# A mixture-of-experts step loop: one transfer for the first rows, shared layer 2 code, thin third tiles as fp32 column tiles, a width of 288

## The chip, the cores and the metric

The kernel runs on one core of one Trainium2 chip. The metric is the device time of one execution in microseconds (us). Five engines work at the same time and wait for each other on semaphores: TensorE (PE in the profile, PEld for its weight loads), VectorE (DVE), ScalarE (ACT), GpSimd (POOL) and SyncE (SP), which issues most transfers.

## The reference

```python
def reference(q, k, v, w_gate, w1, w2):        # 8 batches, 8 heads, 576 positions, 64 wide
    q_s = softmax(q, axis=-1); k_s = softmax(k, axis=2)
    kv = einsum('bhsd,bhse->bhde', k_s, v)
    x = einsum('bhsd,bhde->bhse', q_s, kv)     # then reshaped to 4608 rows x 512
    logits = x @ w_gate                        # 8 experts
    expert_idx = argmax(logits, axis=1)
    gate = softmax(logits)[arange, expert_idx]
    for e in range(8):                         # each row goes to one expert
        y[rows of e] = maximum(x[rows of e] @ w1[e], 0) @ w2[e]    # 512 -> 1024 -> 512
    return gate[:, None] * y
```

## The kernel before

The first 160 us compute the attention, batch by batch, and send every row with its gate and its number to a list in DRAM, `xs`, in which each expert has a region of its own. This part is written out by hand in `ORDER`; its last entries, `WE`, are matmuls on constants (L708) that keep TensorE running until the engines meet before the expert part.

The expert part works in steps of up to three tiles of 128 rows. In each step layer 1 (L1038) makes 8 blocks of 128 hidden units, 12 matmuls each, as wide as the step has rows; layer 2 (L1054) makes, tile by tile, 24 matmuls of 128x512. Both split every fp32 factor in a high and a low part and sum three products, so that each matmul takes one pass. ACT makes the high part of the hidden units from PSUM (`relus`, L1201), DVE the low part (`lows`, L1284). Once per expert ACT and DVE split the weights: W1 (L1240, L1325) in the last step of the expert before, W2 (L1208, L1287) in its own first step. Each finished tile is scaled by ACT (`yout`, L1192) and scattered by POOL (L1371).

The first 384 rows of expert 0 are done by code of their own (`first_l1` L740, `first` L1100). While it runs, POOL scatters the rows of the last batch one after another (L632), with a pause between; when they have landed, SP loads the rows of the first step of the loop (`xload`, L1430), and TensorE turns them (L1023) between the second and third tile of `first`. DVE meanwhile makes a table of the steps (`t5`, 41 small instructions); the other engines and SP read it as they walk over the steps, TensorE as it walks over the experts.

Counted on the inputs, the experts get 1150, 0, 542, 34, 595, 578, 0 and 1709 rows. The order of the loop is expert 0 (766 rows left), 7, 4, 5, 2, 3, then the two empty ones. A remainder of one or two full tiles and a thin one is done as a step of two tiles, 256 wide, and a last step of three tiles whose width goes by the rows of the third: 320 for up to 64 of them, else 352. So the loop has five steps of 384; then 256 and 320 for expert 7 (45 rows in the third tile), 256 and 352 for experts 4 (83) and 5 (66), 256 and 320 for expert 2 (30); and expert 3, with 34 rows, alone in a step of its own, `slim`. `slim` takes the fp32 factors unsplit and works in two column tiles of 64: its layer 2 (L1087) is 16 matmuls of 128x64 by 128x256, 32 in the profile, since each shows as two.

TensorE's loop (`pe_expert`) reads three fields of the table for an expert (`x.get`, L1009) and branches to one of five copies of the step's code, each with its own layer 2. After `slim` it still looks at the two empty experts (`again`, L1124).

SP (`body`, L1469 ff.) loads ahead: the rows of the step after next (`bload`), and in the first step of an expert the weights of the next one: W1 as soon as its room is free (L1465), W2 when the split of the old W2 is done (L1469, which waits on `sW2`).

Of the kernel before, what the change touches and what calls it, by code (L numbers as in the profile page):

```python
# [32 lines left out]
WARM_END = 10  # L33
# [20 lines left out]
L3 VG VH T0 L3 T1 PU L1 VL R5 RB RC RC L2 L3 L1 R5 RB RD RH RH RD L2 L3 PU PU WE WE WE WE WE WE WE WE WE WE  # L54
# [47 lines left out]
def attention_moe(ctx: ExitStack, tc: tile.TileContext, q, k, v, w_gate, w1, w2, xs, out):  # L102
# [35 lines left out]
    I0.GA = cst.tile([P, 3], F32, name="ga")  # L138
    I0.IX = cst.tile([P, 3], I32, name="ix")
# [100 lines left out]
    qthr = cst.tile([E, 2], F32, name="qthr")  # L240
# [15 lines left out]
    def consts():  # L256
# [17 lines left out]
        iota(qthr, pattern=[[Q, 2]], base=-2 * Q, channel_multiplier=0)  # L274
# [477 lines left out]
    def switch():  # L752
        ka.__exit__(None, None, None)
        right.pool = tc.tile_pool(name="it", bufs=1, side="right")
        it = right.it = right.pool.__enter__()
        W2H[0] = it.tile([P, NF, DM], F32R, name="w2h0")
        W2L[0] = it.tile([P, NF, DM], F32R, name="w2l0")
        hid = it.tile([P, 2, NF, 3 * P], F32R, name="hid")
        I0.HH, I0.HL = hid[:, 0], hid[:, 1]
        I0.RAW2 = it.tile([P, NF, DM], F32, name="raw2")  # L760
        I0.YT = [it.tile([P, DM], F32, name=f"yt{i}") for i in range(3)]
        I0.GS = it.tile([P, 3, 2], F32, name="gs")

    def tables():
# [3 lines left out]
        base, start, steps, total, cnt, tiles, threes, rank, own, ends, few, tiny = [  # L768
            small(name, [E, 1]) for name in ("base", "start", "steps", "total", "cnt", "tiles", "threes", "rank", "mykey", "ends", "few", "tiny")]
# [29 lines left out]
        MADE = 41  # L799

        def t5(sem):
# [24 lines left out]
            op('quarter', 'fill', lambda: STT(junk[:, 6, :2], qthr, 1.0, wide(fill, 2), op0=ALU.mult, op1=ALU.is_lt, accum_out=quarter))  # L826
# [6 lines left out]
            op('cut', 'big quarter', lambda: STT(cut, quarter, 2.0, big, op0=ALU.is_lt, op1=ALU.mult))  # L833
# [3 lines left out]
            op('on', 'at', lambda: TS(on, at, 0.0, None, op0=ALU.is_ge))  # L837
            op('last', 'cut quarter', lambda: STT(last, quarter, 1.0, cut, op0=ALU.add, op1=ALU.mult))
            op('tiny', 'few start', lambda: TS(tiny, start, 0.0, 3.0, op0=ALU.is_gt, op1=ALU.mult))
# [15 lines left out]
            op('F9', 'V1 V2 V3 V4 eq', lambda: TT(fld[:, 3 * MAXS:].rearrange("p (a w) -> p a w", a=NFLD), eq[:, None, :].to_broadcast([E, NFLD, TW]), V[:, :, None].to_broadcast([E, NFLD, TW]), op=ALU.mult))  # L855
            op('F0', 'on tiny', lambda: STT(part(fld, 0), on, tiny, part(fld, 0), op0=ALU.mult, op1=ALU.add))
# [62 lines left out]
    def first_gate():  # L919
        TS(I0.GA, XT[:, :, DM], EPS, None, op0=ALU.add)  # L920
        nc.vector.reciprocal(I0.GA, I0.GA)

    add("IM", y, 0, DVE, first_gate, [("IL", y, 0)])
    add("IN", y, 0, POOL, lambda: nc.gpsimd.tensor_copy(I0.IX, XT[:, :, DM + 1]), [("IL", y, 0)])
# [21 lines left out]
    with tc.tile_pool(name="qs", bufs=1, space=PSUM) as qs, tc.tile_pool(name="bx", bufs=1) as bx:  # L946
        I0.XB, I0.XX = bx.tile([P, 12, P], F32, name="xb"), bx.tile([P, NC, 12, 32], F32, name="xx")
        I0.RAW1 = bx.tile([P, NC, F], F32, name="raw1")
        I0.XG, I0.GN, I0.EP = [bx.tile([P, 3, 2], F32, name=n) for n in ("xg", "gn", "ep")]
# [16 lines left out]
def experts(nc, tc, g):  # L966
# [22 lines left out]
    sTH, sTQ, sTY, sTO, sTI, sTG, sXD, sTI2, sTZ = [sem(x) for x in ("sth", "stq", "sty", "sto", "sti", "stg", "sxd", "sti2", "stz")]  # L989
# [27 lines left out]
    def pe():  # L1017
# [42 lines left out]
        def step(w, tiles=3):  # L1060
            layer1(w)
            for u in range(tiles):
                layer2(u)

# [26 lines left out]

        def first(u):
# [19 lines left out]
        e.wait_ge(sX, 48)  # L1112
        for u in (2, 1, 0):
            tr(u, u == 0)
        e.wait_ge(sTC, 1)
        first(2)
        n, i, m2 = x.reg("n", 0), x.reg("i", 0), x.reg("m2", 0)

        def again(name, done=1):
            if done:  # L1120
                x.add("it", 1)
            x.add("n", 1)
            x.add("m2", 16)
            e.br_lt(n, E, "pe_expert", name)  # L1124
            at(name)
            e.br("pe_done")

        e.br("pe_expert")
        with nc.body("pe_expert", valid_engines=[e.engine]):
            body = nc.cur_bb  # L1130
            at = lambda name: nc.switch_bb(name, parent=body)
            r = e.snap(n, min_val=0, max_val=E - 1)
            wide = x.get(WIDE, r, 0, MAXS)
            rest = x.get(REST, r, 0, 5)
            small = x.get(SMALL, r, 0, 4)
            e.reg_mov(i, 0)
            e.br_cond(wide < 1, "pe_rest", "pe_full")
            at("pe_full")
            e.br("pe_wide")
            at("pe_wide")  # L1140
            step(3 * P)
            x.add("it", 1)
            x.add("i", 1)
            e.br_lt(i, wide, "pe_wide", "pe_wide_end")
            at("pe_wide_end")
            e.br("pe_rest")
            at("pe_rest")
            e.br_cond(rest < 1, "pe_none", "pe_some")
            at("pe_none")
            again("pe_out0", 0)  # L1150
            at("pe_some")
            e.br_cond(small < 1, "pe_last", "pe_small")
            at("pe_small")
            e.br_cond(small < 3, "pe_short", "pe_slim")
            at("pe_slim")
            slim()
            again("pe_out4")
            at("pe_short")
            step(2 * P, 1)
            e.br_cond(small < 2, "pe_small_end", "pe_second")  # L1160
            at("pe_second")
            layer2(1)
            e.br("pe_small_end")
            at("pe_small_end")
            e.br_cond(rest < 2, "pe_again", "pe_more")
            at("pe_again")
            again("pe_out1")
            at("pe_more")
            x.add("it", 1)
            e.br("pe_last")  # L1170
            at("pe_last")
            e.br_cond(rest < 4, "pe_320", "pe_352")
            at("pe_320")
            step(2 * P + 2 * Q)
            again("pe_out2")
            at("pe_352")
            step(2 * P + 3 * Q)
            again("pe_out3")
        nc.switch_bb("pe_done")

    def act():
# [6 lines left out]
        def yout(u, again=True):  # L1188
# [3 lines left out]
            m = e.activation(g.YT[u], g.PY[u], AF.Copy, scale=g.GA[:, u:u + 1]).wait_op(sPY[u], cu[u], GE)  # L1192
# [6 lines left out]
        def relus(split):  # L1199
            for f in range(NF):  # L1200
                e.activation(g.HH[:, f, :], g.PH[f][:, :W], AF.Relu).wait_op(sPH[f], it, GE).then_inc(sHH[f], 1)  # L1201
# [18 lines left out]
        def body(j):  # L1220
            kind = x.get(KD, j, 0, 4)
            with e.If(kind > 3):
                slim()
            with e.If(kind < 4):
                usual(j, kind)

        def usual(j, kind):
# [20 lines left out]
            with e.If(kind > 2):  # L1248
                yout(2)
# [15 lines left out]
    def dve():  # L1265
        x = Eng(nc.vector, "dve")
        e = nc.vector
        it, n1, n2, b80 = x.reg("it", 1), x.reg("n1", 1), x.reg("n2", 1), x.reg("b80", 84)

        def flip():  # L1270
            e.wait_ge(sXL, it)
            e.wait_ge(sGS, it)
            e.transpose(g.XX, g.XB.rearrange("p t (a c) -> p c t a", c=NC)).wait_op(sB, b80, GE)  # L1273
            e.tensor_tensor(g.GN, g.XG, g.EP, op=ALU.add).then_inc(sBT, 1)
            x.add("b80", 80)

        def evac():
            e.tensor_tensor(g.XL, xx, g.XH.bitcast(F32), op=ALU.subtract).wait_op(sXH, it, GE).then_inc(sXL, 1)
            e.reciprocal(g.GS[:, :, 0], g.GN[:, :, 0])
            e.tensor_copy(g.GS[:, :, 1], g.GN[:, :, 1]).then_inc(sGS, 1)  # L1280
# [19 lines left out]
        def body(j):  # L1300
            kind = x.get(KD, j, 0, 4)
            with e.If(kind > 3):
                slim()
            with e.If(kind < 4):
# [43 lines left out]
        e.memset(g.EP[:, :, 1], 0.0).then_inc(sB, 1)  # L1348
# [5 lines left out]
        e.tensor_tensor(g.GN, g.XT[:, :, DM:DM + 2], g.EP, op=ALU.add).wait_op(sB, 4, GE).then_inc(sEP, 1)  # L1354
# [176 lines left out]
```

## Time and profile before

| | |
|---|---|
| median of 3 runs | 582.86 us (582.41 to 583.08) |
| the profiled execution | 583.25 us, of which the span from its first to its last instruction is 581.5 us |
| TensorE busy | 553.1 us of the span |
| VectorE, ScalarE, GpSimd busy | 311.0, 245.1, 148.7 us |
| expert loop in the chain that ended last | from 187.26 us to the end |

The chain is the work that ended last, followed back step by step; an engine that stands in it from end to end sets the time there. The rows themselves stand in a section below.

### The profile page before, as it was taken

The page shows a single profiled execution, that of the slowest core. Times are in us where ns is not written, and L with a number is a line of the kernel's source. Part 1 is how long each engine was busy: PE and PEld are TensorE (multiplying, and loading weights), DVE is VectorE, ACT ScalarE, POOL GpSimd, SP SyncE. Part 2 cuts the span into 40 slices and gives each one's busy share as a digit, 9 for nine tenths or more (in the row PEclk, how much of TensorE's full clock was granted, in tenths as well). Part 3 has the DMA queues.
Part 4 walks back from the last instruction along what each step waited for, and adds up shares of the span by engine and source line. Part 5 has one row for each costly group of instructions (what it writes and reads, how often), then busy time and mean ns, then how long its engine had stood idle before and what let it go on. Part 6 is the DMA issues. An engine that isn't in the chain of part 4 may idle for free.

```text
span 581.5 us, 11677 instructions
## 1 busy us (share of the span) xinstructions
PE 553.1 (95%) x3880; PEld 490.6 (84%) x3881; DVE 311.0 (53%) x637; ACT 245.1 (42%) x498; POOL 148.7 (26%) x237
## 2 busy tenths in 40 slices
PE   6699898999998999999999999999999999999995
PEld 2577787898887989899898989898999889898983
DVE  5899997897671431635223242345735472745340
ACT  0699987787321222434131222242625242443331
POOL 4224698586651010110201001102010200110021
PEclk9799998999999999999999999999999999999998
DMA  8989999754568922072504011212570464054000
GB/s 282 315 265 318 322 343 372 244 186 154 205 240 241 268 57 52 12 217 92 167 0 90 18 34 58 60 33 72 187 199 0 121 233 108 18 174 178 18 36 9
DMA packets 64848, 87.21 MB, mean 150 GB/s; under 512 B 8750, under 2 KB 50222, under 8 KB 64176
## 3 DMA queue, kind: packets, MB, share of 16 engines
q1 hardware_dynamic: 58272, 66.70, 37.7%
q0 software_dynamic: 5968, 19.03, 8.8%
q10 hardware_dynamic: 576, 1.07, 0.5%
q8 instruction: 19, 0.31, 0.2%
q14 instruction: 13, 0.11, 0.1%
HBM read 64.83 MB, written 22.61 MB: 150 GB/s over the span
## 4 chain that ended last, share of the span: by engine, by line
PE 82%; DMA 6%; ACT 3%; DVE 2%; issue 2%; POOL 2%; SPq 1%; POOLq 0%; DVEq 0%; ACTq 0%
PE py L1054 33%; PE pt L1038 16%; PE ph L1038 16%; PE xp L512 4%; DMA vs<-in_v 3%; PE kv L375 3%; PE qT L494 2%; PE ph L740 2%; DMA kt<-in_k 1%; PE py L1100 1%; DMA xs<-xr,posi 1%; DMA xt<-xs 1%; PE xp L515 1%; PE pt L1087 1%; ACT vt L178 1%
## 5 line engine op out<-in xcount | busy, mean ns | idle before, releaser
L1054 PE MATMUL py<-w2h,hid 128*128 128x512 f32 x560 | 174.7, 389 | 0.0
L1054 PEld LDWEIGHTS py<-w2h,hid 128*128 128x128 f32 x560 | 105.2, 188 | 21.5
L1371 POOL DMA_INDIRECT out<-yt,ix x38 | 42.6, 1122 | 309.5 <-ACT yt L1192 303.8
L1054 PE MATMUL py<-w2l,hid 128*128 128x512 f32 x280 | 109.1, 390 | 0.0
L1284 DVE SCALAR_TENSOR_TENSOR hid<-pt,hid 128x384 fp32r<-128x384 f32 x52 | 28.8, 556 | 127.4 <-ACT hid L1201 127.2
L1192 ACT ACTIVATE yt<-py,ga 128x512 f32<-128x512 f32 x38 | 26.1, 687 | 139.8 <-PE py L1054 131.0
L1054 PEld LDWEIGHTS py<-w2l,hid 128*128 128x128 f32 x280 | 52.6, 188 | 10.6
L1284 DVE SCALAR_TENSOR_TENSOR hid<-ph,hid 128x384 fp32r<-128x384 f32 x52 | 29.0, 557 | 54.0 <-ACT hid L1201 54.0
L1201 ACT ACTIVATE hid<-ph 128x384 fp32r<-128x384 f32 x52 | 25.6, 492 | 60.2 <-PE ph L1038 60.2
L1201 ACT ACTIVATE hid<-pt 128x384 fp32r<-128x384 f32 x52 | 25.5, 491 | 59.7 <-PE pt L1038 46.9
L1273 DVE STREAM_TRANSPOSE xx<-xb 128x1536 f32<-128x1536 f32 x13 | 37.8, 2906 | 18.3 <-issue 18.3
L512 PE MATMUL xp<-kx,qTs 128*128 128x146 f32 x256 | 45.0, 318 | 2.5 <-ACT kx L413 2.4
L632 POOL DMA_INDIRECT xs<-xr,posi x36 | 37.7, 1047 | 25.0 <-issue 22.8
L512 PEld LDWEIGHTS xp<-kx,qTs 128*128 128x128 f32 x256 | 37.0, 199 | 5.5 <-ACT kx L413 2.9
L1038 PE MATMUL pt<-xh,w1h 128*128 128x384 f32 (+3 forms) x208 | 40.0, 314 | 0.0
L1038 PE MATMUL ph<-xl,w1h 128*128 128x384 f32 (+3 forms) x208 | 39.8, 313 | 0.0
L1038 PE MATMUL pt<-xl,w1h 128*128 128x384 f32 (+3 forms) x208 | 39.8, 313 | 0.0
L1038 PE MATMUL ph<-xh,w1h 128*128 128x384 f32 (+3 forms) x208 | 39.8, 313 | 0.0
L1038 PE MATMUL ph<-xh,w1l 128*128 128x384 f32 (+3 forms) x208 | 39.8, 313 | 0.0
L1038 PE MATMUL pt<-xh,w1l 128*128 128x384 f32 (+3 forms) x208 | 39.8, 313 | 0.0
L1038 PEld LDWEIGHTS pt<-xh,w1h 128*128 128x128 f32 x208 | 33.6, 189 | 1.6 <-issue 0.8
L1038 PEld LDWEIGHTS ph<-xh,w1h 128*128 128x128 f32 x208 | 33.4, 189 | 0.0
(258 smaller groups left out, 925.0 us busy)
## 6 DMA issues: line engine op xcount, KB each, us to landing
raw<-in_moe_w SPq DMA_DIRECT2D x10, 2048.0 KB, 8.2
kt<-in_k SPq DMA_DIRECT2D x14, 640.0 KB, 11.6
xb<-xs SPq DMA_DIRECT2D x32, 192.0 KB
qt<-in_q SPq DMA_DIRECT2D x8, 640.0 KB, 9.1
vs<-in_v SPq DMA_DIRECT2D x8, 640.0 KB, 7.9
qt<-in_q SPq DMA_DIRECT2D x8, 512.0 KB
vs<-in_v SPq DMA_DIRECT2D x8, 512.0 KB, 7.3
xt<-in_moe_w SPq DMA_DIRECT2D x8, 256.0 KB, 6.5
```

The lines of the kernel that those rows point to most:

```text
L375: nc.tensor.matmul(o.kv[i * D:(i + 1) * D, c, lo:lo + D + 1], o.kt[:, 2 * c + i, j, :], VT[b % 2][:, 2 * c + i, at:at + D + 1], start=Fals ...
L494: nc.tensor.transpose(qT[:, c, :], src[:, 2 * c:2 * c + 2, :].rearrange("p h d -> p (h d)"), ident)
L512: nc.tensor.matmul(xv[:, c, :KW], o.qT[i][:, c, :], kx[:, c, :], **flags)
L632: s = nc.gpsimd.indirect_dma_start(out=xs, out_offset=bass.IndirectOffsetOnAxis(ap=n.pi[:, t - t0:t - t0 + 1], axis=0), in_=xr[:, t, :], i ...
L740: m = nc.tensor.matmul(ph, wt[:, c, f * P:(f + 1) * P], xt[:, c, :], start=(n == 0), stop=(n == 3 * NC - 1))
L1038: m = e.matmul(ph, wt[:, c, f * P:(f + 1) * P], xt[:, c, :w], start=(n == 0), stop=(n == 3 * NC - 1))
L1054: m = e.matmul(g.PY[u], ht[:, f, u * P:(u + 1) * P], wt[:, f, :], start=(n == 0), stop=(n == 3 * NF - 1))
L1192: m = e.activation(g.YT[u], g.PY[u], AF.Copy, scale=g.GA[:, u:u + 1]).wait_op(sPY[u], cu[u], GE)
L1201: e.activation(g.HH[:, f, :], g.PH[f][:, :W], AF.Relu).wait_op(sPH[f], it, GE).then_inc(sHH[f], 1)
L1273: e.transpose(g.XX, g.XB.rearrange("p t (a c) -> p c t a", c=NC)).wait_op(sB, b80, GE)
L1284: e.scalar_tensor_tensor(g.HL[:, f, :], g.PH[f][:, :W], 0.0, g.HH[:, f, :].bitcast(F32), op0=ALU.max, op1=ALU.subtract).wait_op(sHH[f], it ...
L1371: e.indirect_dma_start(out=g.out, out_offset=bass.IndirectOffsetOnAxis(ap=g.IX[:, u:u + 1], axis=0), in_=g.YT[u], in_offset=None, bounds_c ...
```

## The change

The last `WE` matmuls are halved, from 10 to 5. SP loads the first step's rows in one transfer, with the row number read before it waits. TensorE waits for the table earlier and reads it ahead of the turning of these rows; in the loop it reads the next expert's three fields in each step, behind the first tile of layer 2. The loop has one copy of layer 2, to which the layer 1 of every width jumps. A third tile with up to 64 rows (`thin`) is done like `slim`'s layer 2: unsplit fp32 hidden units `HF`, which ACT copies in every step (128x64, 8 times), by an unsplit copy of W2, `RAWC`, which SP loads for each expert in its first step, ahead of the next expert's weights; its rows are scattered as halves. A width of 288 is added for up to 32 rows in the third tile. After `slim` TensorE is done. Two instructions are added to `t5`.

```diff
-WARM_END = 10
+WARM_END = 5
...
+            op('thin', 'cut quarter', lambda: STT(thin, quarter, 2.0, cut, op0=ALU.is_lt, op1=ALU.mult))
...
+            op('F0', 'F2 thin', lambda: STT(part(fld, 0), part(fld, 2), thin, part(fld, 0), op0=ALU.mult, op1=ALU.add))
...
+        def thin():
+            e.wait_ge(sYT[2], cu[2])
+            x.add("c2", 1)
+            e.wait_ge(sRC, m3)
+            n = 0
+            for f in range(NF):
+                for d in range(2):
+                    m = e.matmul(g.PY[2][d * SLIM:(d + 1) * SLIM, :DM // 2], g.HF[:, f, :], g.RAWC[:, f, d * DM // 2:(d + 1) * DM // 2],
+                                 start=(f == 0), stop=(f == NF - 1))
+            m.then_inc(sPY[2], 1)
...
+            at("pe_two")
+            layer2(0)
+            nxt = val(n, E - 1)
+            for r, (_, row, hi) in zip(nexts, FIELDS):
+                e.reg_mov(r, x.get(row, nxt + 1, 0, hi))
+            e.br_cond(val(left, 4) < 2, "pe_stepped", "pe_second")
+            at("pe_second")
+            layer2(1)
+            e.br_cond(val(left, 4) < 3, "pe_stepped", "pe_third")
+            at("pe_third")
+            e.br_cond(val(left, 4) < 4, "pe_thick", "pe_thin")
+            at("pe_thick")
+            layer2(2)
+            e.br("pe_stepped")
+            at("pe_thin")
+            thin()
+            e.br("pe_stepped")
...
+            at("pe_288")
+            e.reg_mov(left, 4)
+            e.reg_mov(rest, 0)
+            layer1(2 * P + Q)
+            e.br("pe_two")
...
             at("pe_slim")
             slim()
-            again("pe_out4")
+            e.br("pe_done")
...
+                e.activation(g.HF[:, f, :], g.PH[f][:, 2 * P:2 * P + SLIM], AF.Relu).wait_op(sPH[f], it, GE)
+                e.activation(g.HH[:, f, :], g.PH[f][:, :W], AF.Relu).then_inc(sHH[f], 1)
...
+        def cload(eo):
+            c = e.dma_start(g.RAWC, w2v[bass.ds(eo * NF, NF)].rearrange("c p f -> p c f"))
+            c.wait_op(sW2[NQ - 1], it, GE)
+            c.then_inc(sRC, 16)
...
+                now = e.snap(k, min_val=1, max_val=E - 1)
+                with e.If(x.get(KD, j, 0, 5) < 5):
+                    e.wait_ge(sRC, m3)
+                    x.add("m3", 16)
+                    cload(x.get(EO, now, 0, E - 1))
...
+        row = x.get(ROW, 0, 0, E * RS)
         e.wait_ge(sPad, 16 * E)
         e.wait_ge(sPU, 16 * len(g.late.behind))
-        xload(0)
+        e.dma_start(g.XT, g.xs[bass.ds(row, 3 * P), :].rearrange("(u p) d -> p u d", p=P)).then_inc(sX, 16)
```

On SP, behind the waits for the scatters and the pads, stood before the first of three equal pieces (`tab` is the table, `xt` the first step's rows):

```order
L1009 TENSOR_LOAD tab
L1009 ISA x2
L1009 TENSOR_LOAD tab
L1009 ISA x2
L1429 COMPARE_AND_BRANCH
L1430 ISA
L1430 DMA xt<-xs 128x520
```

and there stands now, with the waits between the last load's rows and the transfer's:

```order
L878 DMA xs<-zr 128x520
L1014 TENSOR_LOAD tab
L1014 ISA x2
L1549 ISA
L1549 DMA xt<-xs 128x3x520
```

The table loads have moved ahead of the waits, or are gone; one transfer is left behind them.

On TensorE, between the first and the second tile of layer 2 (`py` is a tile's PSUM, a number in a name a buffer), stood in the step of 256:

```order
L1054 MATMUL py_2445<-w2l_2144,hid 128x512
L1054 MATMUL py_2445<-w2h_2143,hid 128x512
L1160 COMPARE_AND_BRANCH
L1006 REGISTER_ALU
L1054 MATMUL py_2446<-w2h_2143,hid 128x512
```

and there stands now, for all steps, from the end of the second of three loads on:

```order
L1151 ISA
L1014 TENSOR_LOAD tab
L1014 ISA x2
L1151 ISA
L1152 COMPARE_AND_BRANCH
L1011 REGISTER_ALU
L1059 MATMUL py_2445<-w2h_2144,hid 128x512
```

The three loads have come here from the head of `pe_expert`, where they stood once per expert.

On TensorE, at the end of the step of 320, stood the way back to that head:

```order
L1054 MATMUL py_2447<-w2l_2144,hid 128x512
L1054 MATMUL py_2447<-w2h_2143,hid 128x512
L1006 ISA
L1124 COMPARE_AND_BRANCH
L1126 UNCONDITIONAL_BRANCH
```

and now stands, from the end of a full third tile to the choice of the next expert:

```order
L1160 UNCONDITIONAL_BRANCH
L1011 REGISTER_ALU
L1099 MATMUL py_2446<-rawc,hf 64x256 x16
L1163 UNCONDITIONAL_BRANCH
L1011 ISA
L1166 COMPARE_AND_BRANCH
L1168 UNCONDITIONAL_BRANCH
L1170 COMPARE_AND_BRANCH
L1172 COMPARE_AND_BRANCH
L1011 ISA
L1179 COMPARE_AND_BRANCH
```

The thin tile's 16 matmuls have come in between, and behind them follow branches without a load.

## Rows read from the trace of the kernel before

**Rows 1.** The page's first, second and third part: TensorE, its clock, code packets.

```profile
PE 553.1 (95%) x3880; PEld 490.6 (84%) x3881; DVE 311.0 (53%) x637; ACT 245.1 (42%) x498; POOL 148.7 (26%) x237
...
PEclk9799998999999999999999999999999999999998
...
q8 instruction: 19, 0.31, 0.2%
```

**Rows 2.** The chain that ended last, its front: start us, us, engine, line.

```profile
157.17 2.19 PE hote L708 x10
...
167.75 5.22 DMA xs<-xr,posi
176.11 3.92 DMA xt<-xs
180.07 1.71 PE pt L1023 x12
```

**Rows 3.** The same chain in the expert loop.

```profile
352.33 4.31 PE pt L1038 x36
...
374.76 5.28 PE pt L1038 x36
...
388.84 16.34 PE py L1054 x72
405.18 4.39 PE pt L1038 x36
...
513.79 4.46 PE pt L1038 x36
...
571.37 3.67 PE pt L1087 x32
```

**Rows 4.** Waits of SP, 150 to 200 us: us in total, times, longest.

```profile
SPq L961 <- PE hote L708: 1.1, 1, 1.1
SPq L961 <- DVE hid L748: 0.2, 1, 0.2
```

**Rows 5.** Timeline of 156 to 182 us: start us, us, engine, line.

```profile
174.43 2.02 SPq L1430 DMA_DIRECT2D xt<-xs  x3
...
177.80 0.39 PE L1100 MATMUL py<-w2h,hid 128*128 128x512 f32 x1
```

**Rows 6.** Tile `xt` around the first step's rows, three transfers of 128x520: landings.

```profile
DMA to landing us min/median/max: 2.8/3.1/3.9
```

**Rows 7.** Tile `raw`, the experts' weights, transfers of 128x4096: landings.

```profile
DMA to landing us min/median/max: 7.4/8.2/15.7
```

**Rows 8.** Lines L1124 (395 to 410 us), L1006 (570 to 575 us) and L1087.

```profile
L1124 PEldq COMPARE_BRANCH  x1: 209/209/209, 401.1 to 401.1; - x1
...
L1006 PEldq FUSED_REGOPS  x1: 51/51/51, 572.7 to 572.7; - x1
...
L1087 PE MATMUL pt<-raw,ht x32: 379/379/430, 571.3 to 574.6; 128*64 128x256 f32 x32
```

**Rows 9.** Timeline of TensorE at the start of expert 4.

```profile
405.02 0.71 PE L1038 MATMUL pt<-xh,w1h 128*128 128x256 f32 x4
```

**Rows 10.** Line L961, where the engines meet at the end: ns, start us.

```profile
L961 ACTq DRAIN  x1: 8/8/8, 579.4 to 579.4; - x1
L961 PEldq DRAIN  x1: 8/8/8, 579.7 to 579.7; - x1
```

**Rows 11.** Timeline of ACT in the steps of expert 4.

```profile
415.37 0.49 ACT L1201 ACTIVATE hid<-ph 128x384 fp32r<-128x384 f32 x1 [0.43 <-PE ph L1038]
...
444.96 3.89 ACT L1240 ACTIVATE w1h<-raw 128x1024 fp32r<-128x1024 f32 x4
```

**Rows 12.** Timeline of SP: two weight loads in the first step of expert 4.

```profile
408.09 0.36 SPq L1465 DMA_DIRECT2D raw<-in_moe_w  x1
418.57 0.38 SPq L1469 DMA_DIRECT2D raw<-in_moe_w  x1
```

More of the change, by code (lines that the diff above doesn't have):

```diff
@@ L767, in tables @@
         V = small("V", [E, NFLD])
-        base, start, steps, total, cnt, tiles, threes, rank, own, ends, few, tiny = [
-            small(name, [E, 1]) for name in ("base", "start", "steps", "total", "cnt", "tiles", "threes", "rank", "mykey", "ends", "few", "tiny")]
+        base, start, steps, total, cnt, tiles, threes, rank, own, ends, few, tiny, thin = [
+            small(name, [E, 1]) for name in ("base", "start", "steps", "total", "cnt", "tiles", "threes", "rank", "mykey", "ends", "few", "tiny", "thin")]
         key = small("key", [E, E])
@@ L1111, in pe @@
         cu = [x.reg(f"c{u}", 2) for u in range(3)]
-        e.wait_ge(sX, 48)
+        e.wait_ge(sTC, 1)
+        n, m2, m3 = x.reg("n", 0), x.reg("m2", 0), x.reg("m3", 16)
+        wide, small, rest, left = [x.reg(k, 0) for k in ("wide", "small", "rest", "left")]
+        FIELDS = ((wide, WIDE, MAXS), (rest, REST, 7), (small, SMALL, 5))
+        for r, row, hi in FIELDS:
+            e.reg_mov(r, x.get(row, 0, 0, hi))
+        e.wait_ge(sX, 16)
         for u in (2, 1, 0):
             tr(u, u == 0)
-        e.wait_ge(sTC, 1)
@@ L1116, in pe @@
         first(2)
[L1117 to L1121, printed above, removed]
+        nexts = [x.reg(k, 0) for k in ("nwide", "nrest", "nsmall")]
+        for r, (_, row, hi) in zip(nexts, FIELDS):
+            e.reg_mov(r, x.get(row, 1, 0, hi))
+        val = lambda r, hi: e.snap(r, min_val=0, max_val=hi)
+        e.br("pe_pick")
+        with nc.body("pe_pick", valid_engines=[e.engine]):
+            body = nc.cur_bb
+            at = lambda name: nc.switch_bb(name, parent=body)
+            e.br_cond(val(wide, MAXS) > 0, "pe_full", "pe_rest")
+            at("pe_full")
+            x.add("wide", -1)
+            e.reg_mov(left, 3)
+            layer1(3 * P)
+            e.br("pe_two")
+            at("pe_two")
+            layer2(0)
+            nxt = val(n, E - 1)
+            for r, (_, row, hi) in zip(nexts, FIELDS):
+                e.reg_mov(r, x.get(row, nxt + 1, 0, hi))
[11 more added lines that the diff above has]
+            e.br("pe_stepped")
+            at("pe_stepped")
+            x.add("it", 1)
+            e.br_cond(val(wide, MAXS) > 0, "pe_again", "pe_rest")
+            at("pe_again")
+            e.br("pe_full")
+            at("pe_rest")
+            e.br_cond(val(small, 5) < 1, "pe_over", "pe_some")
+            at("pe_over")
+            e.br_cond(val(rest, 7) < 2, "pe_next", "pe_last")
+            at("pe_next")
@@ new lines, in pe @@
+            for (r, _, _), v in zip(FIELDS, nexts):
+                e.reg_mov(r, v)
+            e.br_lt(n, E, "pe_pick", "pe_last_one")
+            at("pe_last_one")
+            e.br("pe_done")
+            at("pe_some")
+            e.br_cond(val(small, 5) < 3, "pe_short", "pe_slim")
+            at("pe_short")
+            e.reg_mov(left, small)
+            e.reg_mov(small, 0)
+            layer1(2 * P)
+            e.br("pe_two")
+            at("pe_last")
+            e.br_cond(val(rest, 7) < 4, "pe_288", "pe_broad")
@@ L1155, in pe @@
+            e.br("pe_two")
             at("pe_slim")
             slim()
-            again("pe_out4")
[L1158 to L1169, printed above, removed]
@@ L1403, in usual @@
             with e.If(kind > 2):
-                send(2)
+                with e.If(kind > 3):
+                    thin()
+                with e.If(kind < 4):
+                    send(2)
         for i, put in enumerate(g.late.behind):
```

171 lines of the change are left out of this document (80 added, 91 removed).

## The prediction

> **What bounds the kernel now.** [...] Then the chain of work that ended last: from the turning of the first step's rows at 180.07 us on, one TensorE piece follows the other. The expert loop is TensorE's to the end of `slim`, and what its matmuls lose or gain there is the time. Ahead of the loop the chain is another one [rows 2]: the last warm-up matmuls (157.17), POOL's scatters to the last landing (167.75 + 5.22 = 172.97), the load of the rows (landed 176.11 + 3.92 = 180.03), TensorE. So there are three places: the front, the loop, the end. What lies on ACT, DVE and the queues counts only where it makes TensorE wait.
>
> The pace of the loop comes from the chain [rows 3]. 36 matmuls of layer 1 take 4.31 us at width 256 and 5.28 at 320, 120 and 147 ns each. Layer 2 takes 16.34 us for 72, 227 ns each, 5.45 us for a tile.
>
> **The front.** Ten warm-ups take 2.19 us, 0.219 each, and SP, at whom all engines meet, waits 1.1 us for them and for DVE only 0.2 before that [rows 2, 4]. DVE is done by then, so five fewer let all engines start 5 x 0.219 = 1.1 us earlier: **-1.1**. What bounds the front next is POOL's row of scatters, which moves along.
>
> After the last landing SP needs 1.46 us, for two table loads and a branch, to issue the first of three transfers at 174.43; the third is issued at 176.11 [rows 2, 5]. Now only a register instruction and the transfer stand behind the wait: between nothing and 1.46 us, I take 0.2, so the one transfer goes out at 172.97 - 1.1 + 0.2 = 172.1. It holds 3 x 128 rows of 520 fp32, 780 KB. The trace has no such size; below it lie the 260 KB of one piece, 2.8 us at best and 3.1 in the median, above it the 2048 KB of a weight, 8.2 in the median [rows 6, 7]. On the line through both medians 780 KB take 3.1 + 5.1 x 520 / 1788 = 4.6 us: landed at 176.7. TensorE's last matmul ahead of it starts at 177.80 [rows 5], so it is free at 177.80 + 0.23 - 1.1 = 176.9. The wait is gone and the turning starts at 176.9 in place of 180.07. Beyond the 1.1 that is **-2.0**, which TensorE caps. With 2.8 us it is the same; with 8.2 the rows land at 180.3, and it is +1.3. The three table loads that TensorE now makes ahead of this wait run while its queue still holds matmuls of `first`.
>
> **The thin tiles.** Two of the four steps with a remainder have at most 64 rows in the third tile, 45 and 30 by the count of rows. Each loses 24 matmuls, 5.45 us, and gets the list that `slim` runs in L1087, of the same shapes. That list takes 3.67 us in the chain, and its 32 records start from 571.3 to 574.6 [rows 3, 8]; the next tile can follow at that pace, so it occupies TensorE for 3.3 us. 2 x (5.45 - 3.3) = **-4.3**. The bounds are 3.3 and 3.67.
>
> Behind it is a loss. TensorE's sequencer, which handles branches and table loads, runs ahead of the matmuls. At the start of expert 4 it leaves the last step at 401.1 us, and the first matmul of the next one starts at 405.02 [rows 8, 9]; in these 3.9 us it passes three loads and five branches, and the first 36 matmuls lose only 4.39 - 4.31 = 0.08 [rows 3]. So it has a lead of about 3.8 us, 16 or 17 matmuls of 227 ns. Behind `slim`'s list it is at 572.7 with matmuls starting to 574.6 [rows 8]: the same number, but a lead of 1.9 us, since they are shorter. After a thin tile it has eight branches (0.21 us for the one in [rows 8]) and a dozen register instructions, no load: an estimate of 8 x 0.21 + 12 x 0.08 = 2.6 us, the 0.08 from sharing out what the loads and branches leave of the 3.9. 2.6 - 1.9 is 0.7, and 0.1 for the array to empty: 0.8 us after each of the two, **+1.6**. Bounds: nothing if the queue holds more, 3.9 - 1.9 = 2.0 each, +4.0, if the path is as long as with loads.
>
> **The width of 288** is halfway between 256 and 320: (5.28 - 4.31) / 2 x 96 / 36 = **-1.3** for the one step, expert 2's, that gets it. Bounds 0 and -2.6.
>
> **The loop's code.** The table loads leave the expert starts: expert 5's and 2's lost up to 0.15 (4.46 against 4.31), together **-0.2** (expert 4's is in the sum above). They come back behind the first tile of every step, 13 times, where the lead is 3.8 us and three loads and one branch are less than the path that cost 0.08: 0, with 13 x 0.15 = +2.0 as the upper bound. The jump from layer 1 back to the shared layer 2 meets a lead of 16 x 0.12 = 1.9 us at least: 0; its rival is below.
>
> **The end.** ACT is through at 579.4 us, TensorE, with two empty experts to look at, at 579.7 [rows 10]. Without that look ACT is last: **-0.3**.
>
> **What is hidden.** ACT's eight copies `HF` cost between nothing and the 0.49 us of the 128x384 one; in the tightest steps, with the split of W2 between, ACT idles 0.43 us for each block [rows 11]. I take 0. At 0.49 it would be half a microsecond late after eight blocks, and the last block is needed only 7/8 of a tile, 4.8 us, later. SP's copy of W2 waits for the split of the old one, 418.57 in expert 4's first step, and the next W1, issued at 408.09 before, now waits behind it [rows 12]. Two of these loads in a row land after 15.7 us at most [rows 7], so W1 is there at 434.3; ACT takes it at 444.96 [rows 11]: 10 us to spare. Behind the same wait stands SP's next turn, the rows of the step after next; its transfers follow the three loads and land by 451.4 if all four take 8.2 us each (418.57 + 4 x 8.2), and the step that uses them begins at 458 (405.18 + 96 x 0.120 + 2 x 5.45 + 96 x 0.147 + 16.34, from [rows 3], as it was before). DVE has to turn them ahead of that, so here the margin is about 6 us. The two added instructions of the table and DVE's few memsets lie under TensorE's `first`.
>
> **The sum.** -1.1 - 2.0 - 4.3 + 1.6 - 1.3 - 0.2 - 0.3 = -7.6. From the profiled execution's 583.25 us that is 575.65; its time is 0.4 above the median of the runs, so I say **575.3 us** for the median.
>
> **The rivals.**
> *Code that must be fetched* (slower). Layer 1 of every step that isn't 384 wide now ends with a jump far back to the shared layer 2, eight times, with 1.9 us of lead. If each jump waited for a transfer of code as long as the shortest of [rows 6], 2.8 us, and 0.2 for the branch, it would cost 1.1: +8.8, 584.1. It turns the result from a transfer of 2.65 us on. Against it: the page counts 19 packets of code on the queue q8 in the whole run [rows 1], and the start of expert 4, with jumps back over the whole loop, lost 0.08 us. [...] 4%.
> *The two column tiles don't overlap.* Then a thin tile takes twice 3.3, 6.6 us, and the two cost +2.3 in place of -4.3: 581.9, no change that can be told. The rows of `slim`, the same list, speak against it; but there nothing else ran behind. 3%.
> *The one transfer is no faster.* Landing at 179 to 180 in place of 176.7: 577.5 to 578. For it: three small ones may share what one large one needs. 12%.
> *No gap after the thin tiles*: 573.7. For it: the lead is read from one place each. 12%.
> *Loads in each step are seen*, up to +2.0: 576 to 577.3; within the forecast's own range. *No thin tile is taken at all*, because the table's new field doesn't reach the steps: the front, the end, 288 and the loads are left, -4.9, 578.0; 2%.
>
> **How the numbers follow.** The forecast, all terms within a microsecond or two in sum, 574.2 to 577.3, has 64%. With the transfer that is no faster and the missing gap that makes 88%; their outer edges and the gap's upper bound (+2.4 over my value, 577.7) give the range 573.0 to 578.5. It leaves out the code fetch, the tiles without overlap and 3% for what I don't see. A change of 0.2%, 1.2 us, can be told in this kernel. Faster than 581.7: 64 + 12 + 12 + 2 and most of the unseen, 92%; the same 3%; slower 5%.
>
> **What would show it.** The 2 us that TensorE waited for `xt` gone, and the turning near 177; warm-ups 5 and all starts 1.1 earlier; two groups of 32 short matmuls `py<-rawc,hf` of 3.3 us, each followed by an idle weight load of 0.7 to 1 put down to issue; 36 matmuls at 288 in 4.8 us; no idle time at the first matmuls of layer 2; ACT the last to meet at the end. Wrong: idle time ahead of L1059, or W1's split (ACT) waiting for a transfer.

## The result, and the profile after

The changed kernel took 575.87 us in the median of 4 runs (572.40 to 576.22), beside 582.63 us for the kernel before; the ratio is 0.9875, 95% interval 0.9848 to 0.9902. Run again on one chip beside the kernel before, it took 574.29 us (6 runs) against 582.72 (11 runs), 0.9864 (0.9836 to 0.9892). The forecast was 575.3, range 573.0 to 578.5.

Single runs of one kernel differ by up to 7 us here, and the profiles show where much of it lies. In the profiled executions of this study the first warm-up began anywhere from 154.3 to 158.9 us; for the changed kernel alone it was 157.5 in one profile and 155.8 in another. That is the attention part. From there on the two executions of one kernel that were profiled agree to 0.02 us in the loop and the end, and to 0.15 or 0.7 us ahead of it, so each kernel is best read in stages. The table is read from the timelines: when the first warm-up starts, from there to the first matmul behind the engines' meeting, on to the first turning of `xt`, on to the first matmul of the loop, on to the start of `slim`'s last matmul, and on to the end of the span.

| kernel | first warm-up | to meeting | to turning | to loop | loop | end | median of runs |
|---|---|---|---|---|---|---|---|
| before | 157.03 | 3.19 | 19.86 | 7.02 | 387.54 | 6.83 | 582.63 to 583.18 |
| changed | 157.51 | 1.98 | 17.95 | 7.04 | 383.01 | 6.40 | 575.87 |
| changed, second run | 155.82 | 1.98 | 17.80 | 7.04 | 383.03 | 6.40 | 574.29 |
| before, five warm-ups | 158.85 | 1.98 | 20.67 | 8.63 | 387.44 | 6.64 | 583.11 |
| before, one transfer | 156.74 | 3.19 | 17.84 | 7.04 | 387.53 | 6.84 | 579.51 |
| before, both of these | 156.82 | 1.98 | 18.08 | 7.01 | 387.47 | 6.64 | 578.60 |
| changed, three transfers | 155.16 | 1.99 | 17.96 | 7.05 | 383.02 | 6.40 | 573.55 |
| changed, 288 made 320 | 155.97 | 2.00 | 18.46 | 7.04 | 384.46 | 6.42 | 576.23 |
| changed, no thin tiles | 155.00 | 1.98 | 17.77 | 6.98 | 385.92 | 6.41 | 575.94 |
| changed, loads late | 154.30 | 1.99 | 18.10 | 7.03 | 397.74 | 6.39 | 587.67 |
| changed, loads twice | 158.05 | 1.98 | 17.82 | 7.05 | 397.67 | 6.41 | 588.45 |
| changed, early choice | 155.44 | 1.98 | 17.75 | 6.99 | 382.29 | 6.40 | 572.87 |
| the same, second run | 157.54 | 1.99 | 18.46 | 7.04 | 382.29 | 6.41 | 573.35 |

From the first warm-up to the end of the span the change takes off 1.21 + 1.91 + 4.53 + 0.43 - 0.02 = 8.06 us; the attention part began 0.48 later in that profile, so the span fell by 7.6, from 581.5 to 573.9.

The page of the changed kernel, first, second and third part (answering [rows 1]):

```profile
span 573.9 us, 12179 instructions
...
PE 544.8 (95%) x3891; PEld 482.7 (84%) x3892; DVE 314.1 (55%) x644; ACT 256.3 (45%) x602; POOL 147.7 (26%) x237
...
PEclk9799999999999999999999999999999999999998
...
q8 instruction: 19, 0.31, 0.2%
```

TensorE is still busy in 95% of the span; the 8 us are TensorE work and TensorE waits that are gone. ACT has 11 us more; it now makes the copies `HF`. The packets of code are 19, as before.

Its chain of work that ended last (start us, us, engine, line; answering [rows 2, 3]):

```profile
157.66 1.11 PE hote L708 x5
...
166.33 11.11 PE py L1111 x48
177.43 0.01 issue
177.45 1.71 PE pt L1028 x12
...
184.65 6.27 PE pt L1043 x36
...
358.39 2.88 PE ph L1043 x24
361.27 10.91 PE py L1059 x48
...
386.26 10.92 PE py L1059 x48
397.19 3.60 PE py L1099 x32
400.79 0.25 issue
401.04 4.55 PE pt L1043 x36
...
532.22 4.74 PE pt L1043 x36
...
555.78 3.60 PE py L1099 x32
559.38 0.21 issue
559.59 1.95 PE pt L1072 x16
```

In the front the chain no longer goes through POOL, the landing and the transfer: TensorE runs from the second tile of `first` into the turning without a wait. At 361.27 it runs from layer 1 into the shared layer 2 without one, and so at all eight such places of the chain. The two thin tiles, L1099, take 3.60 us each and have 0.25 and 0.21 us of idle time behind them.

The transfer of the first rows in the changed kernel, and the line at which the engines meet at the end (answering [rows 6, 10]):

```profile
L1549 SPq DMA_DIRECT2D xt<-xs x1: 424/424/424, 172.7 to 172.7; - x1
...
DMA to landing us min/median/max: 4.7/4.7/4.7
```

```profile
L966 PEldq DRAIN  x1: 2383/2383/2383, 565.5 to 565.5; - x1
...
L966 ACTq DRAIN  x1: 8/8/8, 572.2 to 572.2; - x1
```

The rows land at 172.7 + 4.7 = 177.4, just as TensorE gets there. At the end ACT is the last to meet, and TensorE, through with its program at 565.5 and with its matmuls 2.4 us later, is not.

TensorE's sequencer in the step of 320 (compare [rows 8]): the three loads behind the first tile, the branch behind them, and behind the thin tile the first branch and the last move.

```profile
L1014 PEldq TENSOR_LOAD <-tab x3: 298/298/310, 387.7 to 389.2; - x3
...
L1152 PEldq COMPARE_BRANCH  x1: 76/76/76, 390.0 to 390.0; - x1
```

```profile
L1166 PEldq COMPARE_BRANCH  x1: 210/210/210, 398.7 to 398.7; - x1
...
L1186 PEldq MOVE  x1: 35/35/35, 400.8 to 400.8; - x1
```

The loads begin at 387.7 and the branch is passed at 390.1, while the first tile's matmuls run to 391.7 (half of the 10.92 us behind 386.26): 4.0 us of lead, 2.4 of them used. The way back behind the thin tile takes from 398.5 (0.2 ahead of that branch) to 400.9, 2.4 to 2.5 us, while the tile's matmuls run to 400.79: a lead of 2.3 us, just too little.

### The profile page after: what moved, and what is told of

Its sections match the earlier page's. It is cut to its first block, busy times and chain, and to the rows that moved or that the text cites. A ratio compares the mean times of both kernels' runs of the same rounds, so it can differ in the third digit from the quotient of the medians.

```text
span 573.9 us, 12179 instructions
## 1 busy us (share of the span) xinstructions
PE 544.8 (95%) x3891; PEld 482.7 (84%) x3892; DVE 314.1 (55%) x644; ACT 256.3 (45%) x602; POOL 147.7 (26%) x237
## 4 chain that ended last, share of the span: by engine, by line
PE 75%; issue 0%; POOL 0%; ACT 0%; DVE 0%; POOLq 0%; SPq 0%
PE py L1059 31%; PE pt L1043 16%; PE ph L1043 16%; PE py L1111 3%; PE ph L740 3%; PE py L1099 1%; PE xp L512 1%; PE pt L1087 1%; PE qT L494 0%; PE pt L740 0%; PE pt L1072 0%; PE ph L1072 0%; PE pt L1028 0%; PE pt L726 0%; PE xp L515 0%
## 5 line engine op out<-in xcount | busy, mean ns | idle before, releaser
L1225 ACT ACTIVATE yt<-py,ga 128x512 f32<-128x512 f32 (+1 forms) x38 | 25.7, 678 | 134.0 <-PE py L1059 120.0
L1043 PE MATMUL pt<-xh,w1h 128*128 128x384 f32 (+4 forms) x208 | 39.8, 313 | 0.2 <-issue 0.2
L1043 PE MATMUL ph<-xh,w1h 128*128 128x384 f32 (+4 forms) x208 | 39.6, 312 | 0.0
L1043 PE MATMUL pt<-xl,w1h 128*128 128x384 f32 (+4 forms) x208 | 39.6, 312 | 0.0
L1043 PE MATMUL ph<-xh,w1l 128*128 128x384 f32 (+4 forms) x208 | 39.6, 312 | 0.0
L1043 PE MATMUL pt<-xh,w1l 128*128 128x384 f32 (+4 forms) x208 | 39.6, 312 | 0.0
L1043 PE MATMUL ph<-xl,w1h 128*128 128x384 f32 (+4 forms) x208 | 39.5, 312 | 0.0
L1234 ACT ACTIVATE hf<-pt 128x64 f32<-128x64 f32 x52 | 11.7, 225 | 55.8 <-PE pt L1043 43.3
L1234 ACT ACTIVATE hf<-ph 128x64 f32<-128x64 f32 x52 | 11.7, 224 | 53.0 <-PE ph L1043 53.0
L1043 PEld LDWEIGHTS pt<-xl,w1h 128*128 128x128 f32 x208 | 33.3, 189 | 0.0
```

The lines of the kernel that those rows point to most:

```text
L1043: m = e.matmul(ph, wt[:, c, f * P:(f + 1) * P], xt[:, c, :w], start=(n == 0), stop=(n == 3 * NC - 1))
L1225: m = e.activation(g.YT[u][:, :w], g.PY[u][:, :w], AF.Copy, scale=g.GA[:, u + thin:u + thin + 1]).wait_op(sPY[u], cu[u], GE)
L1234: e.activation(g.HF[:, f, :], g.PH[f][:, 2 * P:2 * P + SLIM], AF.Relu).wait_op(sPH[f], it, GE)
```

## The experiments

**Five warm-ups alone.** The kernel before with

```diff
-WARM_END = 10
+WARM_END = 5
```

> The kernel before with five warm-up matmuls in place of ten, nothing else. My theory: the engines' meeting is released by the last warm-up, so TensorE's first matmul behind it comes 1.1 us earlier, counted from the first warm-up (3.19 us before, 2.1 then), and as POOL's scatters and the three transfers move along, the turning of the first rows comes 21.9 to 22.0 us after the first warm-up (23.04 before): 581.5 us. Rival A, DVE's last low part is the one that releases: 0.2 us less at most, 582.4. Rival B, the scatters' landing doesn't move: the turning stays at 23.0 us behind the first warm-up, 582.6.

583.11 us (12 runs) against 583.18 (20 runs): 0.9984, 0.9962 to 1.0006, nothing that can be told. The meeting comes 1.21 us earlier, as said, but the turning is not: the three transfers go out 14.9 us behind the meeting, 14.2 before, and TensorE, which comes to them earlier, waits longer. And the stretch behind the turning takes 8.63 us in place of 7.02. The timeline of that wait in the kernel before, and here (the idle time and what ended it in brackets):

```profile
180.07 1.71 PE L1023 MATMUL pt<-ident,xt 128*128 128x128 f32 x12 [1.88 <-DMA xt<-xs]
```

```profile
181.50 1.91 PE L1023 MATMUL pt<-ident,xt 128*128 128x128 f32 x12 [2.72 <-DMA xt<-xs]
```

And the windows behind it, of before, then of this kernel (stretch, us, busy us of PE, PEld, DVE, ACT and POOL with their counts, then the granted clock, the DMA share and GB/s):

```profile
182.00:184.00 2.00, 2.00 (x11) 1.62 (x10) 0.69 (x1) 1.86 (x2) 0.00 (x0) 1.00 1.16 184
```

```profile
183.00:185.00 2.00, 2.00 (x7) 1.61 (x7) 0.07 (x1) 1.55 (x2) 0.00 (x0) 0.50 1.19 191
185.00:186.50 1.50, 1.50 (x6) 1.17 (x5) 1.50 (x1) 0.48 (x1) 0.13 (x1) 0.57 1.32 215
186.50:190.00 3.50, 3.50 (x17) 2.88 (x16) 0.50 (x4) 0.00 (x0) 0.87 (x1) 1.00 0.88 365
```

Behind 2.72 us without work the granted clock is 0.50 from 183.00 to 185.00 and 0.57 from there to 186.50; behind the 1.88 of the kernel before it is 1.00 from 182.00 to 184.00. In this execution all of the gain went into the later landing and the clock. Rival B has the better of it here, for a reason that neither theory had. The other eleven runs have no trace, and the interval of the times, from 2.2 us less to 0.3 more, leaves room for the whole 1.2 us.

**One transfer alone.** The kernel before with

```diff
+        row = x.get(ROW, 0, 0, E * RS)
         e.wait_ge(sPad, 16 * E)
         e.wait_ge(sPU, 16 * len(g.late.behind))
-        xload(0)
+        e.dma_start(g.XT, g.xs[bass.ds(row, 3 * P), :].rearrange("(u p) d -> p u d", p=P)).then_inc(sX, 16)
```

> The kernel before with the one transfer for the first step's rows and its row number read ahead of the wait; ten warm-ups, TensorE's own order unchanged. My theory: the rows land before TensorE is through with the second tile of its first step, so from its first matmul behind the meeting to the turning it takes 17.9 to 18.0 us in place of 19.85, and the time is 580.6. Rival, the transfer is no faster than three: only the loads and the issues are saved, the rows land a microsecond later than TensorE is free, 18.8 to 19.4 us and 581.6 to 582.2.

579.51 us (9 runs) against 583.18, 0.9945 (0.9923 to 0.9967). From the meeting to the turning it takes 17.84 us in place of 19.86, and TensorE no longer waits for the rows. The theory's 17.9 to 18.0 holds within 0.1.

**Three transfers, without what stood between.** The changed kernel with

```diff
-        e.dma_start(g.XT, g.xs[bass.ds(row, 3 * P), :].rearrange("(u p) d -> p u d", p=P)).then_inc(sX, 16)
+        for u in range(3):
+            e.dma_start(g.XT[:, u, :], g.xs[bass.ds(row + u * P, P), :]).then_inc(sX, 16)
```

> The changed kernel with three transfers of 128 rows again, but issued straight behind the wait, without table loads or branches between. My theory, that the number of transfers counts: SP issues the third 1.0 to 1.7 us after the first and it lands 3 to 3.9 us later, 177.5 to 178.5 where the one landed at 177.4, so TensorE waits 0 to 1 us, most likely 0.6: 576.5 us. Rival, that only the loads and branches ahead of the transfer mattered: no wait at all, 575.9.

No wait at all: 17.96 us to the turning, 17.95 with one transfer, and 573.55 us. My theory fell and its rival holds. The transfers of this kernel:

```profile
L1550 SPq DMA_DIRECT2D xt<-xs x3: 333/360/372, 170.3 to 171.5; - x3
...
DMA to landing us min/median/max: 2.8/3.1/3.6
```

The last of three lands at 171.5 + 3.6 = 175.1, 4.8 us after the first was issued; the one of the changed kernel took 4.7. So merging the transfers gave nothing that can be seen. The gain is from SP's side of the wait: the two table loads and the branch ahead of the first transfer, and the branches between them, which set the three 0.84 us apart before and 0.57 here.

**Both edits of the front,** on the kernel before.

> The kernel before with both edits of the front, five warm-ups and the one transfer with its row number read ahead; its loop is untouched. Theory 1, the five warm-ups failed alone because the three late transfers then set the turning, and with the rows early they bring their 1.2 us: from the first warm-up to the turning 19.9 to 20.4 us in place of 23.05, 3.1 to 2.6 less, 579.9 to 580.4. Theory 2, fewer warm-ups make the scatters land later behind the meeting of the engines by 0.7 us in general: 20.6 to 20.8 us, 580.7 to 581.0.

From the first warm-up to the turning 1.98 + 18.08 = 20.06 us, in place of 23.05: theory 1. The time is 578.60 us against 582.72, 0.9922 (0.9892 to 0.9952). Beside the 3.19 + 17.84 = 21.03 us with one transfer alone, the five warm-ups now bring 0.97 of their 1.2 us. That is read from one profile of each; the two times, 579.51 and 578.60 in different comparisons, can't tell it.

**No warm-ups.** The kernel of the early choice (below) with `WARM_END = 0`.

> The kernel with the early choice behind thin tiles, and no warm-ups at all. Theory 1: with five the last warm-up ends 0.08 us behind DVE's last low part, so without them the meeting comes 0.1 us earlier and no more; TensorE then idles 1.9 us ahead of it, as long as it did once without losing its clock: same time as with five, within 0.2 us from the last matmul of the hidden units ahead of the meeting to the turning. Rival A, warm-ups are what the meeting waits for: 1.1 us less. Rival B, an idle time of 1.9 us here is enough for TensorE to fall to its lower clock, as it did behind 2.7 us: the first matmuls behind the meeting take twice their time for some 3 us, 1.5 us more.

573.60 us, against 573.35 with five in the same comparison. The meeting does not come earlier: from the last small matmul ahead of it to the first behind it 1.99 us, 2.01 in the changed kernel. The first half of theory 1 holds, DVE releases it: in the chain its last low part (157.20 + 0.57) stands straight ahead of the meeting. The second does not: the timeline and a window behind it show

```profile
156.55 0.19 PE L601 MATMUL rk<-oh,ones 128*128 128x16 bf16 x2
158.56 1.32 PE L740 MATMUL pt<-xh,w1h 128*128 128x384 f32 x4 [1.82 <-SPq L966]
159.69 1.48 PE L740 MATMUL pt<-xl,w1h 128*128 128x384 f32 x4
```

```profile
160.00:162.00 2.00, 2.00 (x8) 2.00 (x8) 1.97 (x23) 0.00 (x0) 1.83 (x3) 0.50 0.61 219
```

Behind 1.82 us of idle time the clock is 0.50 from 160.00 to 162.00, and from the meeting to the turning it takes 19.34 us in place of 17.8. Rival B holds for this execution; its time, 575.35, is the longest of its six runs, and whether the clock fell in the others too isn't shown.

**The width.** The changed kernel with `layer1(2 * P + Q)` made `layer1(2 * P + 2 * Q)`.

> The changed kernel with the step of 288 made 320 wide; the thin tile stays. My theory: the 96 matmuls of layer 1 go from 131.7 to 146.7 ns each, 1.4 us more in that step, 577.3 us. Rival: what follows, the thin tile and the slim step, hides part of it: under 0.7 us, 576.5 or less.

The loop takes 384.46 us in place of 383.01, 1.45 more, all of it in that step: the theory. (Its front waited 0.55 us for the rows, which landed later; the time, 576.23 us, holds both.)

**No thin tiles.** The changed kernel with

```diff
-            op('thin', 'cut quarter', lambda: STT(thin, quarter, 2.0, cut, op0=ALU.is_lt, op1=ALU.mult))
+            op('thin', 'cut quarter', lambda: STT(thin, quarter, 0.0, cut, op0=ALU.is_lt, op1=ALU.mult))
...
             at("pe_288")
-            e.reg_mov(left, 4)
+            e.reg_mov(left, 3)
```

and the same in `pe_320`.

> The changed kernel without thin tiles: both third tiles of up to 64 rows are done like the others, 128 wide and split. ACT's copies of the hidden units and SP's loads of the unsplit W2 stay. My theory: the two tiles take 5.45 us again in place of 3.6 and the idle time behind them (0.25 and 0.21 us) goes with the slow start of the next 36 matmuls: 3.0 us more, 578.9. Rival, the copies and loads that came with the thin tile cost time of their own: then more than 3.5 us lies between this kernel and the sum, or idle time stands before matmuls of layer 1 or before ACT's split of W1.

The loop takes 385.92 us, 2.91 more: the theory's 3.0. This kernel still has the copies `HF`, the loads of the unsplit W2 and the width of 288; with the 1.45 us that the width is worth it would take 387.37, not more than the 387.54 of before. So the copies and the loads cost the loop nothing that can be seen. In the time the thin tiles are harder to see: 575.94 us (6 runs) lies 3 us below the 578.9 expected, which was counted from the 575.87 of the first runs. In the same comparison the early choice (below) took 572.87, 3.1 less, where the loops differ by 3.63.

**The loads behind the last tile.** The changed kernel with the three loads of `pe_two` moved to `pe_stepped`:

```diff
             layer2(0)
-            nxt = val(n, E - 1)
-            for r, (_, row, hi) in zip(nexts, FIELDS):
-                e.reg_mov(r, x.get(row, nxt + 1, 0, hi))
...
             at("pe_stepped")
+            nxt = val(n, E - 1)
+            for r, (_, row, hi) in zip(nexts, FIELDS):
+                e.reg_mov(r, x.get(row, nxt + 1, 0, hi))
```

> The changed kernel with the three table loads of each step moved from behind the first tile to behind the last one. My theory, TensorE's sequencer has a lead of 3.8 to 4.2 us behind a full tile and 2.3 us behind a thin one, the way back takes 2.5 us and the three loads 2.4: behind the two thin tiles the idle time grows by 2.4 us each, from 0.25 to 2.6; behind the two steps of 352 by 0.7 to 1.1 each; behind expert 0's last by some 0.5; behind the other full steps and those of 256 nothing. Together 6.5 to 7.5 us, 582.9. Rival A, the lead is no matter and loads always cost their 2.4 us where they stand: they would have cost that already behind the first tile, so nothing changes, 575.9. Rival B, the queue holds far more: nothing either.

587.67 us, and 14.7 us more in the loop: twice what I expected, and both rivals are out. Its chain at expert 7's thin tile and at expert 4's last step:

```profile
396.24 3.60 PE py L1099 x32
399.84 2.85 issue
402.69 5.79 PE pt L1043 x36
...
459.12 1.23 issue
```

and its window behind the first of these:

```profile
402.70:404.50 1.80, 1.80 (x8) 1.80 (x9) 0.00 (x0) 0.00 (x0) 0.00 (x0) 0.50 0.36 92
```

The idle time behind the thin tile grew from 0.25 to 2.85 as the lead has it, and behind the steps of 352 it is 1.2 to 1.3. Two things were missing: the steps of 256 end with a second tile and a way back that is long as well, 0.57 to 0.77 idle in three of four; and behind 2.85 us of idle time the clock is at 0.50 again, so that the next 36 matmuls take 5.79 us in place of 4.55. Behind the second thin tile it is the same: 2.83 us idle, a clock of 0.50 from 569.80 to 572.00, and 3.40 us for 16 matmuls of `slim` in place of 1.95. By these two the clock makes (5.79 - 4.55) + (3.40 - 1.95), some 2.7 of the 14.7 us.

**The loads twice,** behind the first tile (`in 2 * list(zip(nexts, FIELDS))`).

> The changed kernel with each of the three table loads behind the first tile done twice, in all 13 steps. My theory: from the last matmul that it issues to the next the sequencer has 4.2 us; three loads and a branch take 2.6 of it, six take 4.9 to 5.0, so each step loses 0.7 to 0.9 us at the first matmul of the second tile: 9 to 12 us, 586.4. Rival A, a smaller lead than I read, 2.6 us: 2.4 lost in each step, 31 us, 607. Rival B, a larger one: nothing, 575.9.

588.45 us, 14.7 more in the loop, 1.1 per step: the theory by its mechanism, with a size above its range, for the steps are of two kinds. The chain in expert 4's first step and in its second:

```profile
420.12 5.46 PE py L1059 x24
425.59 1.56 issue
427.15 5.73 PE py L1059 x24
...
448.35 5.48 PE py L1059 x24
453.83 0.56 issue
454.39 11.17 PE py L1059 x48
```

and the waits for W2 in layer 2 of these two steps (L1057), the loads (L1014) and the branch behind them (L1152):

```profile
L1057 PEldq EVENT_SEMAPHORE  x4: 51/51/51, 418.2 to 422.1; - x4
...
L1014 PEldq TENSOR_LOAD <-tab x6: 297/309/314, 422.5 to 426.2; - x6
...
L1152 PEldq COMPARE_BRANCH  x1: 76/76/76, 426.9 to 426.9; - x1
...
L1057 PEldq EVENT_SEMAPHORE  x4: 51/51/51, 445.6 to 448.2; - x4
...
L1014 PEldq TENSOR_LOAD <-tab x6: 296/300/308, 449.8 to 453.4; - x6
...
L1152 PEldq COMPARE_BRANCH  x1: 76/76/76, 454.2 to 454.2; - x1
```

In both the next tile's matmuls start 0.2 us behind the branch. In an expert's first step the sequencer stands at the last quarter of W2 until 422.1, so that it starts on the loads at 422.5, 3.1 us ahead of the last matmul's end (425.6); in the second step, where W2 is there, they begin 4.1 us ahead. Four of the 13 steps are of the first kind: those with which experts 7, 4, 5 and 2 begin.

**The choice made early.** The changed kernel with the registers' work and the choice of the next step ahead of the thin tile's matmuls, and one copy of these behind each choice:

```diff
             at("pe_thin")
-            thin()
-            e.br("pe_stepped")
+            e.wait_ge(sYT[2], cu[2])
+            x.add("c2", 1)
+            e.wait_ge(sRC, m3)
+            x.add("it", 1)
+            x.add("n", 1)
...
+            e.br_cond(val(wide, MAXS) > 0, "pe_thin_full", "pe_thin_rest")
...
+            at("pe_thin_short")
+            thin()
+            e.br("pe_short")
+            at("pe_thin_slim")
+            thin()
+            e.br("pe_slim")
```

> The changed kernel with the choice of the next expert's step made ahead of the thin tile's matmuls (one copy of them for each choice), so that one branch and two moves follow them in place of eight branches. My theory, that the idle time behind the thin tile is the sequencer's way back: 0.5 us is under its lead of 2.3, the 0.25 and 0.21 us go, and the next 36 matmuls start at 4.35 in place of 4.55: 575.2 us, 0.5 to 0.7 less. Rival, that it is the change of shape or type in the array: the idle time stays at 0.2 to 0.25 each and the time at 575.9.

572.87 us against 582.97 for before, 0.9841 (0.9811 to 0.9871), and 0.72 us less in the loop than the changed kernel. Its chain behind the two thin tiles:

```profile
398.46 4.51 PE pt L1043 x36
...
553.17 3.60 PE py L1095 x32
556.77 1.73 PE pt L1072 x16
```

The idle time is gone: the 16 matmuls of `slim` follow the thin tile at 553.17 + 3.60. It was the sequencer's. What stays is a slow start of the next step, 4.51 us in the chain for 36 matmuls where 4.32 is usual. Half of that is the chain's way of counting, from the end of the piece before: from the first start to the 37th it is 4.42 (398.39 to 402.81), 0.10 more than the 4.32 at the next expert.

**The two side by side,** for the spread and for the version that came out best.

> The changed kernel as it is, beside the kernel with the early choice on the same chip. Its first run had four times of 572.4 to 576.2, and the first warm-up of the profiled execution 0.5 us later than in the profile of before, from the attention part, which the change doesn't touch. If that start is what spreads the times, the front, the loop and the end take 19.9, 383.0 and 6.4 us again, and the time less the start of the first warm-up is 418.2 us again. If the spread is in the loop or the end, these differ by over 0.3.

> The kernel with the early choice behind thin tiles, beside the changed kernel on the same chip. Its loop took 382.3 us where the changed kernel's took 383.0: 0.7 us less in the median than the run of the changed kernel beside it, if the loop is all that differs; no difference or a slower one if the larger code (four copies of the thin tile's matmuls) costs elsewhere.

The changed kernel's stages repeat to 0.15 us, its first warm-up came 1.7 us earlier: the spread is that of the start. In the time the early choice is 573.35 us against 574.29, which the runs can't tell from nothing; in the loop it is 382.29 against 383.03, as in the first pair. Rows that landed later held TensorE 0.66 us longer in that profile.

## Why the prediction was right, point by point

- **What bounds the kernel.** TensorE at the loop, a chain through POOL and SP ahead of it: so it was. What was taken from TensorE's list came off the time.
- **Warm-ups, -1.1:** 3.19 to 1.98 at the meeting, -1.21. But the term was made as if it stood by itself. Alone it brought nothing that can be told in the times, and in the one trace of it a later landing and the clock of 0.50 took it back. With the rows early 0.97 of it is seen; that it needs them isn't shown beyond these traces.
- **The transfer, -2.0, capped by TensorE:** -1.91, and -2.02 alone. The landing took 4.7 us, the line through two sizes gave 4.6. SP's issue came 0.2 us behind its wait, as taken. The rival *the one transfer is no faster* was right in its mechanism, shown by the three that landed 4.8 us behind the first issue where the one took 4.7, and wrong in its result, since the loads and branches that went with them were the cost.
- **Thin tiles, -4.3 + 1.6 = -2.7:** 2.91 by the experiment. Both terms were mis-sized, in opposite ways. A tile occupies TensorE for 3.60 us and not 3.3, the whole list counts: 2 x (5.45 - 3.60) = 3.70. The loss behind the two is then 3.70 - 2.91 = 0.8 and not 1.6: 0.25 and 0.21 of idle time, and slow starts (4.55 us for the 36 matmuls behind the first of the two, in place of 4.32). (The 0.1 that the forecast took for the array to empty stands in no row, and no run shows it; the runs show 0.25 and 0.21 of idle time as a whole.) The mechanism, that the lead is shorter behind short matmuls, 2.3 us where it was 4.0 behind the first full tile, is shown by the early choice, which took the idle time away, and by the late loads, which lengthened it. Its size was off because the lead is 2.3 us, not 1.9. The rival *no gap* is out, but not by far.
- **288, -1.3:** -1.45.
- **The loads, 0, and -0.2 at the expert starts:** the loop's 4.53 less 2.91 and 1.45 leaves 0.17. The cover is smaller than I said for four of the 13 steps: I read a lead of 3.8 us everywhere, and in the first step of experts 7, 4, 5 and 2 the wait for W2 leaves some 3.1 of it, for a path of 2.4.
- **The end, -0.3:** -0.43, ACT last.
- **Code that must be fetched:** did not come. No idle time stands ahead of the shared layer 2 at any of the eight places, and there are 19 packets of code as before. None of them falls behind 432 us, where five of the eight jumps lie. The 0.08 us that I held against it came from other jumps, for the kernel before has none out of layer 1; that these cost nothing is shown by the eight alone, and for this kernel.
- **What was to be hidden** stayed hidden: in the changed kernel's loop only POOL waits for a transfer, 58.1 us in all for its own scatters, so W1's split was not held up.
- **Column tiles that don't overlap:** out, 3.60 us a tile.

The sum was -7.6; from the first warm-up on it was -8.06, and the profile's own -7.6 is that with 0.48 of a later start: the exact agreement is partly luck. So it is in the thin tiles, where errors of 0.6 and 0.8 us nearly cancelled. That a change of 0.2% can be told was too hopeful: the intervals here reach 0.2 to 0.3% to either side.

## What to carry to other kernels

Read how far TensorE's sequencer is ahead at each place where branches or loads are to stand: the same path was free behind 24 long matmuls, cost 0.25 us behind short ones, and 2.85 with three loads more. Here it was cheaper to make the choice ahead of the short list. Of several transfers behind one wait, look first at what the issuing engine does between the wait and the first of them. A shorter path to a meeting can be worth nothing where a later wait takes it back, as in the trace of the five warm-ups alone, where the idle time there even grew.

## What the runs showed of the hardware that I had not expected

- Idle time cost more than itself. Behind 2.72 us (five warm-ups alone), 2.85 and 2.83 us (late loads) and 1.82 us (no warm-ups) the granted clock was 0.50 in windows of 1.8 to 2.2 us (183.00 to 185.00; 402.70 to 404.50 and 569.80 to 572.00; 160.00 to 162.00), and the stretches with them took 1.2 to 1.6 us more (8.63 - 7.02; 5.79 - 4.55 and 3.40 - 1.95; 19.34 - 17.8). With five warm-ups alone TensorE worked again from 181.50 on; the clock was 0.95 in the mean to 183.00 and 0.50 from there. Behind the 1.88 us of the kernel before it was 1.00. So in these traces the length of the idle time alone does not decide it; what does isn't shown here.
- Behind the thin tile's fp32 matmuls the next 36 took 4.42 us from start to start even without idle time, 0.10 more than usual. The cause was not tried.
- The scatters' landing varies: where no table load stands behind its wait, SP issued the first transfer 13.0 us behind the meeting with ten warm-ups, and 13.1 to 13.9 us with five or none. In the three profiles of 13.5 and above (13.55, 13.70, 13.86) TensorE waited 0.18, 0.55 and 0.55 us; below that it waited 0.12 at most.
